# Linear attention and a gated feed-forward network: the written order of the steps is replaced from step 166 of 594 on

## The chip, the cores and the metric

The kernel runs on one core of one Trainium2 chip. The metric is the device time of one execution in microseconds (us); three runs of the kernel before gave 249.38, 249.55 and 249.58 us, median 249.55. The engines are named as the profile names them: PE (TensorE matmul), DVE (VectorE), ACT (ScalarE), POOL (GpSimd) and SP (SyncE, which here only issues transfers).

## The reference

Eight batches of linear attention with eight heads (576 tokens, head width 64), then a feed-forward network over all 4608 rows:

```python
phi = lambda x: np.where(x > 0, x, np.exp(x) - 1.0) + 1.0
kv  = einsum('bhsd,bhse->bhde', phi(k), v)
z   = sum(phi(k), axis=2)
x   = einsum('bhsd,bhde->bhse', phi(q), kv) / (einsum('bhsd,bhd->bhs', phi(q), z) + 1e-6)
x   = x.transpose(0, 2, 1, 3).reshape(4608, 512)
out = ((x @ w1) * (x @ w2)) @ w3 @ w_out      # w1, w2: 512 x 1024, w3: 1024 x 1024, w_out: 1024 x 512
```

## The kernel before

**Tiles and chunks.** The 576 tokens of a batch are 512 "full" tokens (four tiles of 128) and a tail of 64. The feed-forward part works on chunks of 512 rows: chunk c is the full tokens of batch c (0 to 7), and chunk 8 is the eight tails together. The product of w3 and w_out is made once, at the start, so a chunk needs only the two gate products, their elementwise product and one output product. The last three chunks (6, 8, 7) use a scheme with seven half-size products in place of eight, with more sums on DVE.

**The written order.** The program is not ordered by a scheduler. A string `ORDER` of 594 short steps (line 577 on) is walked once, and `step` turns each into its instructions. Each engine, and each queue of transfers, carries out its own instructions strictly in the order in which they were written, and waits at the first one whose input or buffer isn't ready. A step is a letter, a batch or chunk number, and a part:

- `L`, `M`, `N`: load one half (four heads, 512 KB of f32) of k, q, v of a batch (`load_qkv`, line 104). With a `+` it is issued by POOL, without by SP.
- `R`: load the tails of a batch (`load_tail`, line 114): `R4.0` is four transfers of 64 KB (q and k), `R4.1` two (v). `+` again means POOL.
- `x`/`X`, `y`/`Y`, `z`/`Z`: phi of k / of q, by an exponential on ACT (line 179), a maximum on DVE (line 184) and a minimum on DVE (lines 204, 209).
- `v`: v into bf16 (line 215; tails line 221), on ACT, or on DVE with `+`.
- `K`: the kv product of a batch, 18 matmuls (lines 245, 249) and two copies (line 254) on ACT, or on DVE with `+`.
- `T`: phi(q) turned round by a transposing transfer on SP (line 269). `D`: the same for the attention output of a batch (`D2.0`) or for the tails of two batches (`D1.1`) (line 351).
- `A`: the attention output of 128 tokens (part 4: the tail): four matmuls (line 310), then three instructions on DVE (lines 324 to 326). The four parts 0 to 3 of a batch fill the tile that `D` turns round.
- `F`: one of eight gate units of a chunk: eight matmuls (line 362), a copy on ACT (line 367), a product on DVE (line 368). `G`, `m`, `e`, `d`: the same for chunks 6, 8, 7 in the other scheme (lines 396 to 465).
- `O`: one output tile, eight matmuls (line 536) and a copy (line 538) on ACT, or on DVE with `+`. `S`, `H`: store of finished rows by SP (lines 546, 551). `Q`: the last output tile with its stores.

**Buffers that tie steps together.** `ld` has 13 buffers of one half each; four PSUM buffers serve the gate units (two for each `F`), two serve `O`, and a single one serves `K` and `A`, so that each of these waits until the one ahead of it has been read out. `ldr`, for tails, has three buffers. A transfer also waits for the eighth transfer ahead of it on its own queue to land.

**Gates.** `GATES` adds two waits by hand: `R6.0<T3.0` lets the q and k tails of batch 6 start only when `T3.0` has landed. It stands in both kernels.

```python
    for s in ORDER.split():
        step(s)
```

Of the kernel before, what the change touches and what calls it, by code (L numbers as in the profile page):

```python
# [20 lines left out]
def kernel(  # L21
# [568 lines left out]
    A3.0 O1.2 A3.2 L4.1 v4.2+ F2.6 A3.3 F2.3 N4.1 y4.0 F2.1 M4.0 x4.0 A3.1 x4.1 F2.0 M4.1 y4.2 v5.2+  # L590
    x4.2 F2.7 Y4.0 D3.0 F2.4 z4.0 F2.2 X4.1 Y4.1 S1.0 F2.5 v4.1 Z4.1 N4.0 M5.0 X4.0 Z4.0 A3.4 z4.2
    y4.1 O2.3 F3.7 z4.1 M5.1 v4.0 A2.4 Y5.0 F3.6 L5.0 T4.0 M6.1 R6.0+ x5.2 Y5.1 X5.0 F3.1 N5.1 Z5.0
    S1.1 O2.2+ K4 F3.2 M6.0 x6.2 X5.1 A4.2 Z5.1 F3.4 z5.2 F3.5 y5.0 A4.1 F3.0 L5.1 F3.3 N5.0 y5.1
    X6.1 y6.2 O2.1 A4.3 R6.1+ N6.0 S2.1 x5.1 N6.1 v5.0+ T5.0 O2.0 x5.0 v5.1+ A4.0 R7.0+ z5.1 D4.0
    z5.0 X6.0 O3.3 y7.2 O3.2+ K5+ S2.0 L6.0 z6.2 O3.1 A5.2 L6.1 O3.0 A5.1 D1.1 Y6.1 Z6.1 F4.2 A5.0
    Y6.0 F4.5 y6.1 F4.7 v6.0+ x6.1 L7.0 x6.0 M7.0 A5.3 D3.1 x7.0 z6.1 F4.0 v6.1+ v6.2 F4.6 A4.4 Z6.0
    F4.1 S3.0 F4.4 D5.0 A5.4 y6.0 z6.0 F4.3 M7.1 F5.7 x7.2 y7.0 Y7.0 z7.2 L7.1 N7.0 K6+ z7.0 F5.6
    F5.0 y7.1 X7.1 X7.0 Z7.0 F5.5 S3.1 F5.3 Y7.1 T6.0 R7.1+ Z7.1 A6.3 T7.0 F5.1 O4.2 A6.1 x7.1 O4.1
    A6.2 e1.0 e0.0 v7.0 F5.4 A6.0 z7.1 O4.3 e0.1 F5.2 e1.1 v7.2+ O4.0 N7.1 S4.1 e0.2 e0.3 e1.2 D6.0
    d6.0 v7.1 A6.4 e1.3 O5.1 O5.0 G6.1.1 G6.1.2 d6.1 G6.0.1 K7 d6.2 d6.3 G6.0.2 G6.0.3 m6.1.2 G6.0.4  # L600
    m6.0.2 S5.0 A7.3 G6.1.3 G6.0.5 G6.1.4 G6.1.5 m6.0.5 G6.2.4 G6.0.6 G6.0.7 G6.1.7 A7.0 G6.1.6
    G6.2.1 S4.0 G6.3.1 D5.1 G6.2.2 G6.2.3 G6.3.2 G6.3.3 m6.1.6 G6.2.5 G6.3.4 m6.2.2 G6.3.5 G6.2.6
    G6.2.7 A7.4 D7.1 G6.3.7 G6.3.6 O5.2 m6.3.5 A7.2 d8.0 O5.3 d8.2 G8.0.1 G8.0.4 m6.2.6 d8.1 m6.0.6
    d8.3 A7.1 G8.1.1 m6.3.6 G8.0.3 G8.0.2 G8.1.3 m6.2.5 G8.1.4 G8.0.5 G8.1.5 G8.3.4 G8.1.6 m8.0.2
    G8.0.7 G8.1.7 G8.2.4 m6.1.5 D7.0 G8.1.2 m8.0.5 d7.0 G8.2.1 S5.1 G8.3.1 G8.0.6 G8.2.3 m8.0.6
    G8.2.6 G8.3.3 G8.2.5 m6.3.2 G7.0.4 G8.3.5 G7.1.4 m8.1.2 G8.2.7 d7.1 G8.2.2 G8.3.7 d7.2 m8.1.5
    G8.3.6 O6.0 m8.3.5 m8.1.6 d7.3 O6.3 m8.2.5 O6.2+ m8.3.6 m8.2.6 O6.1 G7.0.1 m8.2.2 G8.3.2 G7.1.1
    m8.3.2 G7.0.3 S6.0 G7.0.6 G7.1.3 G7.0.5 G7.0.2 G7.1.5 G7.3.4 m7.1.5 G7.0.7 G7.2.4 m7.0.6 G7.1.7
    G7.1.6 m7.0.2 G7.2.1 G7.2.2 G7.3.1 S6.1 m7.2.2 G7.2.3 G7.2.6 G7.3.3 G7.2.5 G7.3.6 G7.3.5 G7.2.7
    G7.3.2 G7.1.2 G7.3.7 m7.3.2 m7.3.6 m7.1.2 O8.2 m7.3.5 O8.3 m7.0.5 O7.0 m7.2.6 O7.1 H8.2 m7.2.5  # L610
# [119 lines left out]
```

## Time and profile before

| what | value |
|---|---|
| three runs | 249.38, 249.55, 249.58 us |
| profiled execution, first to last instruction | 248.0 us |
| PE busy | 230.9 us (93%), 1548 matmuls |
| DVE busy | 187.4 us (76%), 434 instructions |
| ACT busy | 131.9 us (53%), 213 instructions |
| POOL busy | 49.4 us (20%) |
| DMA | 49.43 MB, mean 199 GB/s over the span |
| mean granted PE clock | 0.991 |

The profile gives for the profiled execution its span alone, 248.0 us, which is 1.5 us below the median of the runs. Its lines are read thus: a timeline row has the start in us, the duration in us, engine, line and operation, output<-input, the number of instructions merged into it, and in brackets the idle time ahead of it with what ended it. Rows of PE have a modelled end, so two rows that follow each other overlap a little: late matmuls are seen in the distance between starts. A row "SPq" is the time that SP spent in issuing a transfer; when the transfer landed stands in the view of the DMA issues. That view's last lines list, for the transfers issued in a stretch, how many there were, their size and the median time from issue to landing.

### The profile page before, as it was taken

The page shows a single profiled execution, that of the slowest core. Times are in us where ns is not written, and L with a number is a line of the kernel's source. Part 1 is how long each engine was busy: PE and PEld are TensorE (multiplying, and loading weights), DVE is VectorE, ACT ScalarE, POOL GpSimd, SP SyncE. Part 2 cuts the span into 40 slices and gives each one's busy share as a digit, 9 for nine tenths or more (in the row PEclk, how much of TensorE's full clock was granted, in tenths as well). Part 3 has the DMA queues.
Part 4 walks back from the last instruction along what each step waited for, and adds up shares of the span by engine and source line. Part 5 has one row for each costly group of instructions (what it writes and reads, how often), then busy time and mean ns, then how long its engine had stood idle before and what let it go on. Part 6 is the DMA issues. An engine that isn't in the chain of part 4 may idle for free.

```text
span 248.0 us, 4281 instructions
## 1 busy us (share of the span) xinstructions
PE 230.9 (93%) x1548; PEld 133.6 (54%) x1548; DVE 187.4 (76%) x434; ACT 131.9 (53%) x213; POOL 49.4 (20%) x79
## 2 busy tenths in 40 slices
PE   0699868999999999999999999999999999999994
PEld 0445455654454554345445544545488688578542
DVE  3227769777898847788768799988899999779810
ACT  2206667658756725675563383536466377245321
POOL 8546368665014050500000000000000000000000
PEclk9999988999999999999999999999999999999999
DMA  7999999999999999999999999917750133040144
GB/s 159 193 202 310 295 211 211 194 259 288 287 219 329 236 234 273 217 304 282 288 362 268 284 270 221 295 37 174 169 193 0 22 65 107 3 169 1 44 152 145
DMA packets 64021, 49.43 MB, mean 199 GB/s; under 512 B 32480, under 2 KB 58848, under 8 KB 64000
## 3 DMA queue, kind: packets, MB, share of 16 engines
q1 hardware_dynamic: 52928, 36.31, 58.3%
q0 software_dynamic: 10928, 12.72, 25.2%
q8 instruction: 12, 0.20, 0.3%
q10 hardware_dynamic: 144, 0.13, 0.2%
q14 instruction: 9, 0.07, 0.1%
HBM read 38.80 MB, written 9.44 MB: 194 GB/s over the span
## 4 chain that ended last, share of the span: by engine, by line
PE 67%; DMA 21%; ACT 3%; DVE 3%; SPq 2%; issue 2%; POOL 0%; ACTq 0%; DVEq 0%; POOLq 0%
PE o_ps L536 21%; PE a_ps L362 12%; PE b_ps L362 12%; DMA q<-in_q_dram 10%; PE gu L422 9%; DMA w3b<-in_moe_w_dram 7%; PE gt L422 6%; DMA k<-in_k_dram 4%; PE nd L310 3%; PE kvp L245 2%; SPq L104 1%; ACT e L179 1%; PE o_ps L561 1%; PE kvp L249 1%; DVE qj L209 1%
## 5 line engine op out<-in xcount | busy, mean ns | idle before, releaser
L536 PE MATMUL o_ps<-wf_sb,ab 128*128 128x512 bf16 x280 | 64.2, 379 | 0.0
L362 PEld LDWEIGHTS <-w_sb 128*128 128x128 bf16 x384 | 36.5, 98 | 40.6 <-issue 0.8
L362 PE MATMUL a_ps<-xt,w_sb 128*128 128x512 bf16 x192 | 50.3, 379 | 0.5 <-ACT a_sb L367 0.5
L362 PE MATMUL b_ps<-xt,w_sb 128*128 128x512 bf16 x192 | 50.3, 379 | 0.0
L536 PEld LDWEIGHTS <-ab 128*128 128x128 bf16 x280 | 26.8, 98 | 29.3
L368 DVE TENSOR_TENSOR ab<-a_sb,b_ps 128x512 bf16<-128x512 f32 x48 | 32.5, 683 | 11.5 <-PE b_ps L362 5.9
L538 ACT COPY o_sb<-o_ps 128x512 f32<-128x512 f32 x30 | 17.4, 585 | 42.8 <-PE o_ps L536 28.8
L367 ACT COPY a_sb<-a_ps 128x512 f32<-128x512 f32 x48 | 27.7, 585 | 22.2 <-PE a_ps L362 21.8
L326 DVE TENSOR_TENSOR xn<-nd,r 128x512 bf16<-128x512 f32 x30 | 20.7, 691 | 1.0
L422 PEld LDWEIGHTS <-spare 128*128 128x128 bf16 x192 | 18.7, 98 | 2.2
L179 ACT ACTIVATE e<-q 128x1024 bf16<-128x1024 f32 x16 | 16.8, 1057 | 5.7 <-DMA q<-in_q_dram 5.0
L310 PE MATMUL nd<-kv,qt 128*128 128x130 bf16 (+1 forms) x160 | 16.6, 228 | 2.9 <-ACT kv L254 1.8
L179 ACT ACTIVATE e<-k 128x1024 bf16<-128x1024 f32 x16 | 16.8, 1056 | 3.2 <-DMA k<-in_k_dram 3.1
L310 PEld LDWEIGHTS <-qt 128*128 128x128 bf16 (+1 forms) x160 | 11.8, 103 | 12.2 <-issue 3.5
L454 DVE TENSOR_TENSOR spare<-spare,gt 128x512 f32<-128x512 f32 x24 | 16.1, 680 | 1.8 <-PE gt L422 0.9
L154 PE MATMUL wf_ps<-wt_sb,w3t 128*128 128x512 bf16 x64 | 16.5, 403 | 0.6 <-DMA wt_sb<-in_moe_w_out_dram 0.6
L450 ACT COPY spare<-gu 128x512 f32<-128x512 f32 x24 | 13.6, 587 | 3.9 <-PE gu L422 3.7
L422 PEld LDWEIGHTS <-w_sb 128*128 128x128 bf16 x144 | 14.0, 98 | 2.7 <-issue 0.3
L465 DVE TENSOR_TENSOR ab<-spare 128x256 bf16<-128x256 f32 x36 | 14.1, 417 | 0.1
L114 POOL DMA_DIRECT2D qk32r<-in_q_dram x14 | 9.0, 644 | 23.3 <-ACT a_sb L367 10.7
L209 DVE TENSOR_TENSOR qj<-e,y 128x512 bf16<-128x512 bf16 x32 | 12.1, 418 | 2.0 <-ACT e L179 1.8
L422 PE MATMUL gu<-spare 128*128 128x256 bf16 x96 | 13.4, 272 | 0.0
(87 smaller groups left out, 294.0 us busy)
## 6 DMA issues: line engine op xcount, KB each, us to landing
out_dram<-o_sb SPq DMA_DIRECT2D x15, 512.0 KB, 3.9
q<-in_q_dram SPq DMA_DIRECT2D x13, 512.0 KB, 8.1
k<-in_k_dram SPq DMA_DIRECT2D x12, 512.0 KB, 7.0
v<-in_v_dram SPq DMA_DIRECT2D x12, 512.0 KB, 9.0
w3b<-in_moe_w_dram POOLq DMA_DIRECT2D x8, 256.0 KB, 10.0
k<-in_k_dram POOLq DMA_DIRECT2D x4, 512.0 KB, 9.1
w_sb<-in_moe_w_dram POOLq DMA_DIRECT2D x8, 256.0 KB, 7.5
q<-in_q_dram POOLq DMA_DIRECT2D x3, 512.0 KB, 12.6
```

The lines of the kernel that those rows point to most:

```text
L154: nc.tensor.matmul(wfs[i], w3ts[i][:, kc, :], wo_sb[:, kc, :], start=(kc == 0), stop=(kc == FC - 1))
L179: nc.scalar.activation(out=e, in_=x, func=AF.Exp)
L209: nc.vector.tensor_tensor(out=p[0][:, 2 * g + c].rearrange("p j u d -> p u j d"), in0=e[:, c], in1=y[:, c], op=ALU.min)
L310: nc.tensor.matmul(nds[g][rows, i * 2 * E1:(i + 1) * 2 * E1], w, kvs[b % 2][:, i, g].rearrange("p u e -> p (u e)"), start=True, stop=True)
L326: nc.vector.tensor_tensor(out=dst.rearrange("p (g h) e -> p g h e", g=2), in0=v4[:, :, :, 0:D], in1=r[rows].unsqueeze(3).to_broadcast([n, ...
L362: nc.tensor.matmul(ps, w[:, kc, f * P:(f + 1) * P], xt_of(c)[:, :, kc, :], start=(kc == 0), stop=(kc == KC - 1))
L367: nc.scalar.copy(out=a_sb, in_=a_ps)
L368: nc.vector.tensor_mul(out=abs_[c][:, f, :], in0=a_sb, in1=b_ps)
L422: nc.tensor.matmul(t[:, w], l, r, start=(first and w == 0 and k == 0), stop=(k == 1), skip_group_check=True)
L454: nc.vector.tensor_tensor(out=s, in0=o, in1=t, op=ALU.add)
L536: nc.tensor.matmul(o_ps, ab[:, f, m * P:(m + 1) * P], wf_sb[:, f, :], start=(f == 0), stop=(f == FC - 1))
L538: copy_of(alt)(out=rows_of(c, m // 2)[:, m % 2], in_=o_ps)
```

## The change

The first 165 steps stay as they are; they end with `F1.7 F1.6 x2.2`, the first two gate units of chunk 1 and the exponential of a tail. From there on the same 429 steps stand in another order. A few of them also change the engine: on ACT in place of DVE now run `v2.0 v5.0 v5.1 v6.0 v6.1`, the tails `v2.2 v4.2 v5.2 v7.2`, `O1.1` and the copies of `K5` and `K6`; on DVE in place of ACT run `v2.1`, `v3.2`, `v6.2`, `O2.3 O4.2 O5.0 O7.2`; the tails of batch 7 (`R7.0`, `R7.1`, six transfers) are issued by SP in place of POOL. All halves of q, k and v from batch 2 on are issued by SP in both kernels. PE has the same 1548 matmuls. The diff replaces the rows of the table from line 586 on; two of them of before, and two with the change:

```diff
-    A1.4 x2.1 F1.7 F1.6 x2.2 L2.0 y2.1 y2.2 Y2.0 x3.2 R3.1+ X2.0 O0.3 N2.1 x2.0 z2.1 N2.0 y2.0 z2.2
...
-    v3.1 S0.1 A2.1 y3.1 R5.1+ z3.0 z3.1 v3.0 v3.2 O1.1+ O1.0 T3.0 D2.0 S0.0 L4.0 K3 R4.1+ R4.0+ O1.3
...
+    A1.4 x2.1 F1.7 F1.6 x2.2 y2.2 z2.2 N2.1 y3.2 x3.2 O0.3 F1.0 Y2.0 X2.0 Z2.0 N2.0 y2.1 F1.1 v2.1+
...
+    T3.0 A2.1 R6.0+ v3.1 O1.1 z3.0 A2.0 O1.0 D2.0 R4.0+ S1.0 z3.1 K3 O1.2 A3.0 O1.3 A3.3 F2.5 F2.3
```

Three places of the order, engine by engine. Numbers behind a name tell buffers of one program apart, and are not the same in the two programs.

SP before, from the transpose of batch 2's attention output (`D2.0`) to that of batch 3 (`D3.0`). The loads are, in turn, both halves of k of batch 4, a half of its v, and both halves of its q:

```order
L351 DMA_TRANSPOSE xt_1149<-xn_1029 128x16x128
L546 DMA out_0_dram<-o_sb_1073 128x1024
L104 DMA k32_1152<-in_k_dram 128x4x256
L104 DMA k32_1223<-in_k_dram 128x4x256
L104 DMA v32_1263<-in_v_dram 128x4x256
L104 DMA q32_1280<-in_q_dram 128x4x256
L104 DMA q32_1308<-in_q_dram 128x4x256
L351 DMA_TRANSPOSE xt_1331<-xn_1195 128x16x128
L546 DMA out_0_dram<-o_sb_1135 128x1024
```

SP with the change, over the same stretch and to the fifth load behind it. The loads ahead of `D3.0` are one half of q of batch 5 and one of batch 4; behind it stand the other half of q of batch 4, a half of its v, both of its k, and the other half of its v:

```order
L351 DMA_TRANSPOSE xt_1142<-xn_1019 128x16x128
L546 DMA out_0_dram<-o_sb_1118 128x1024
L104 DMA q32_1262<-in_q_dram 128x4x256
L546 DMA out_0_dram<-o_sb_1182 128x1024
L104 DMA q32_1288<-in_q_dram 128x4x256
L351 DMA_TRANSPOSE xt_1304<-xn_1185 128x16x128
L104 DMA q32_1310<-in_q_dram 128x4x256
L104 DMA v32_1327<-in_v_dram 128x4x256
L104 DMA k32_1345<-in_k_dram 128x4x256
L104 DMA k32_1361<-in_k_dram 128x4x256
L104 DMA v32_1497<-in_v_dram 128x4x256
```

Five loads and a store stood between the two transposes; now there are two loads and two stores, and four of the five loads of batch 4 that stood there have moved behind the second transpose.

ACT before, from the copies of `O1.3` and `O1.2` through the gate units of chunk 2 (a_sb is the copy of a gate unit, e the exponential of a half, er that of a tail, vt a half of v):

```order
L538 COPY o_sb<-o_ps 128x512 x2
L367 COPY a_sb<-a_ps 128x512 x3
L179 ACTIVATE e<-k_1152 128x1024
L179 ACTIVATE e<-k_1223 128x1024
L367 COPY a_sb<-a_ps 128x512
L179 ACTIVATE er<-qk32r 128x512
L367 COPY a_sb<-a_ps 128x512 x3
L179 ACTIVATE e<-q_1308 128x1024
L367 COPY a_sb<-a_ps 128x512
L215 CAST vt_104<-v_1263 128x4x4x64
L179 ACTIVATE e<-q_1280 128x1024
```

ACT with the change, from the copies of `O1.2` and `O1.3` (the last two rows ahead of the gate units) through chunk 2 and into chunk 3:

```order
L538 COPY o_sb<-o_ps 128x512 x2
L367 COPY a_sb<-a_ps 128x512 x4
L179 ACTIVATE er<-qk32r 128x512
L367 COPY a_sb<-a_ps 128x512 x2
L221 CAST vr_106<-v32r 64x2x2x64 x2
L367 COPY a_sb<-a_ps 128x512 x2
L179 ACTIVATE e<-q_1262 128x1024
L367 COPY a_sb<-a_ps 128x512
L179 ACTIVATE e<-q_1310 128x1024
L179 ACTIVATE e<-q_1288 128x1024
L215 CAST vt_104<-v_1327 128x4x4x64
```

The exponentials of batch 4's halves stood among the eight copies of chunk 2; now only the tails of batch 4 (er and vr) stand there, and the first exponential of a half (one of batch 5's q) comes behind all eight.

POOL, the tails (each row is two transfers, or as many as its last number says). The piece of the difference begins at `R3.0`:

```order
 L114 DMA qk32r<-in_q_dram 64x4x64 x2
 L114 DMA qk32r<-in_k_dram 64x4x64 x2
-L114 DMA v32r<-in_v_dram 64x4x64 x2
-L114 DMA qk32r<-in_q_dram 64x4x64 x2
-L114 DMA qk32r<-in_k_dram 64x4x64 x2
-L114 DMA v32r<-in_v_dram 64x4x64 x6
+L114 DMA v32r<-in_v_dram 64x4x64 x4
 L114 DMA qk32r<-in_q_dram 64x4x64 x2
 L114 DMA qk32r<-in_k_dram 64x4x64 x2
 L114 DMA qk32r<-in_q_dram 64x4x64 x2
 L114 DMA qk32r<-in_k_dram 64x4x64 x2
```

Behind `R3.0` (its first two rows) stood `R3.1 R5.0 R2.1 R5.1 R4.1 R4.0` ahead of the gated `R6.0`; now only `R2.1 R3.1` do, and `R6.0` is followed by `R4.0 R5.1 R4.1 R5.0 R6.1`, which makes 18 transfers that wait behind the gate or are it.

More of the change, by code (lines that the diff above doesn't have):

```diff
@@ L585 @@
     M2.1 M3.1 A1.3 F0.3 P1.3 X2.1 R2.0+ A1.0 L2.1 h0 h1 Y2.1 P1.0 M2.0 h2 h3 Z2.1 i0 i1 X3.1 R3.0+
-    A1.4 x2.1 F1.7 F1.6 x2.2 L2.0 y2.1 y2.2 Y2.0 x3.2 R3.1+ X2.0 O0.3 N2.1 x2.0 z2.1 N2.0 y2.0 z2.2
-    Z2.0 F1.0 M3.0 R5.0+ y3.2 T2.0 v2.1 L3.0 Y3.1 R2.1+ F1.5 N3.1 v2.0+ z2.0 L3.1 Z3.1 v2.2+ O0.2
-    F1.2 F1.1 Y3.0 y5.2 z3.2 K2 F1.4 A2.2 X3.0 F1.3 A2.3 x3.0 O0.1 Z3.0 A2.0 x3.1 N3.0 y3.0 O0.0
-    v3.1 S0.1 A2.1 y3.1 R5.1+ z3.0 z3.1 v3.0 v3.2 O1.1+ O1.0 T3.0 D2.0 S0.0 L4.0 K3 R4.1+ R4.0+ O1.3
@@ L590 @@
[L590 to L610, printed above, removed]
@@ L611 @@
-    H8.3 O8.0 m7.1.6 S7.0 O8.1+ S8.0 O7.2 H7.2 Q7.3
+    A1.4 x2.1 F1.7 F1.6 x2.2 y2.2 z2.2 N2.1 y3.2 x3.2 O0.3 F1.0 Y2.0 X2.0 Z2.0 N2.0 y2.1 F1.1 v2.1+
+    R2.1+ z2.1 L2.0 y2.0 v2.2 F1.5 R3.1+ x2.0 z2.0 M3.0 v2.0 F1.4 O0.2 X3.0 K2 Y3.1 v3.2+ Z3.1 O0.1
+    Y3.0 Z3.0 T2.0 A2.3 F1.2 A2.2 N3.0 F1.3 v3.0 L3.1 z3.2 L3.0 x3.0 x3.1 y3.0 S0.1 y3.1 O0.0 N3.1
+    T3.0 A2.1 R6.0+ v3.1 O1.1 z3.0 A2.0 O1.0 D2.0 R4.0+ S1.0 z3.1 K3 O1.2 A3.0 O1.3 A3.3 F2.5 F2.3
+    A3.2 F2.0 M5.1 Y5.1 R5.1+ R4.1+ y4.2 S1.1 F2.2 M4.1 A3.1 R5.0+ D3.0 x4.2 z4.2 M4.0 F2.1 Y4.1
@@ new lines @@
+    N4.1 F2.4 R6.1+ L4.1 e0.0 A2.4 v4.2 L4.0 F2.6 e0.2 F2.7 X5.1 Z5.1 A3.4 F3.3 X4.0 Y4.0 Z4.0 O2.3+
+    X4.1 y5.2 v4.1 y4.1 F3.1 y6.2 Z4.1 x4.1 F3.4 z4.1 v5.2 y4.0 x4.0 F3.0 N4.0 z4.0 F3.5 v4.0 O2.2+
+    M5.0 X5.0 K4 v6.2+ e0.1 T4.0 F3.7 x5.2 z5.2 L5.1 x5.1 Y5.0 Z5.0 y5.1 F3.2 S0.0 A4.1 F3.6 L5.0
+    y5.0 O2.1 N5.0 x5.0 A4.0 v5.0 O2.0 z5.1 N5.1 S2.1 A4.2 T5.0 v5.1 O3.3 z5.0 A4.3 D4.0 O3.2+ K5
+    S3.1 O3.1 A5.3 M6.1 O3.0 A5.0 F4.0 X6.1 A5.2 F4.7 M6.0 X6.0 Y6.0 Z6.0 D3.1 F4.2 F4.4 A5.1 F4.5
@@ new lines @@
+    e1.0 F4.3 L6.1 y6.1 x6.1 A4.4 R7.0 L6.0 y6.0 y7.2 D5.0 F4.1 x6.0 F4.6 z6.0 Y6.1 Z6.1 F5.6 x6.2
+    z6.2 z6.1 F5.5 N6.1 v6.1 N6.0 A5.4 e1.1 e1.3 M7.0 X7.0 F5.7 S2.0 F5.4 Y7.0 O4.2+ v6.0 K6 O4.3
+    T6.0 A6.3 S3.0 O4.0 A6.1 F5.3 D5.1 x7.2 z7.2 A6.0 M7.1 Y7.1 R7.1 X7.1 Z7.1 N7.0 v7.0 L7.0 F5.1
+    F5.0 A6.2 L7.1 Z7.0 F5.2 x7.1 y7.1 O4.1 y7.0 A6.4 e0.3 x7.0 z7.0 S4.1 z7.1 O5.0+ v7.2 N7.1 v7.1
+    D6.0 d6.2 O5.1 K7 d6.0 d6.1 d6.3 G6.1.1 e1.2 T7.0 G6.0.1 G6.0.2 G6.1.2 m6.0.2 G6.1.3 G6.0.3
+    G6.1.4 A7.3 S4.0 G6.0.4 G6.0.5 G6.1.5 S5.0 G6.2.4 G6.0.6 G6.0.7 G6.1.6 G6.1.7 m6.1.6 A7.0 m6.0.6
@@ new lines @@
+    G6.2.1 G6.2.2 G6.3.1 G6.2.3 G6.3.2 G6.3.3 G6.2.5 G6.3.4 G6.2.6 G6.3.5 G6.2.7 A7.4 G6.3.6 G6.3.7
+    O5.2 m6.3.2 D1.1 A7.2 O5.3 m6.1.2 m6.2.6 D7.1 d8.0 d8.1 d8.3 G8.0.1 G8.0.2 d8.2 A7.1 G8.1.1
+    G8.0.3 m6.3.6 G8.0.4 G8.1.3 G8.0.5 m8.0.5 G8.1.4 m6.2.5 G8.3.4 S5.1 D7.0 G8.1.5 G8.0.7 m6.2.2
+    G8.2.4 G8.0.6 m8.0.6 G8.1.7 O6.0 m6.3.5 m6.1.5 m6.0.5 O6.3 d7.2 G8.2.1 G8.2.2 m8.2.2 d7.0 G8.3.1
+    G8.2.3 G8.1.6 G8.3.3 G8.2.5 G8.3.2 G7.0.4 G8.3.5 G8.2.7 G8.3.6 m8.3.6 m8.1.6 G7.1.4 G8.3.7
+    m8.0.2 O6.2+ S6.1 d7.1 d7.3 O6.1 S6.0 m8.2.5 G7.0.1 m8.3.5 G8.1.2 m8.1.5 m8.1.2 G7.1.1 G7.0.3
@@ L612 @@
+    G7.0.6 G7.1.3 G7.0.5 G7.2.4 G7.1.5 G8.2.6 G7.0.7 G7.1.6 G7.1.7 G7.0.2 m8.2.6 m8.3.2 m7.1.6
+    G7.2.1 G7.2.2 G7.3.1 G7.2.3 G7.3.2 m7.0.5 G7.3.4 G7.3.3 G7.2.5 G7.3.6 G7.3.5 G7.2.7 G7.1.2
+    G7.2.6 G7.3.7 m7.0.2 m7.2.5 O8.2 O8.3 m7.3.2 H8.3 m7.3.5 m7.2.2 O8.0 m7.1.2 m7.0.6 O8.1+ H8.2
+    S8.0 O7.0 O7.1 S7.0 m7.2.6 m7.3.6 m7.1.5 O7.2+ H7.2 Q7.3
     """
```

## The prediction

> **What bounds the kernel now.** I read the busy times by stage first, then the chain of waits, then the rows around each gap of PE. By stage (length, PE, PE's weight loads, DVE, ACT, POOL with their counts, granted clock, DMA share, GB/s):
>
> ```profile
> 60.00:95.00 35.00, 35.00 (x209) 17.71 (x208) 26.69 (x65) 21.73 (x35) 8.61 (x14) 1.00 1.09 261
> 95.00:130.00 35.00, 33.80 (x185) 16.02 (x184) 28.05 (x63) 21.44 (x32) 3.94 (x6) 1.00 1.10 289
> 130.00:243.00 113.00, 112.99 (x774) 70.64 (x775) 94.64 (x215) 56.23 (x100) 0.00 (x0) 1.00 0.54 138
> ```
>
> From 60 us on, where the new order begins, PE is never idle but for 1.2 us between 95 and 130. PE keeps its 1548 matmuls, so a new order can save what PE loses here and no more, while it can lose any amount. The chain of waits leaves PE only where it lies on loads:
>
> ```profile
> 91.59 12.85 DMA q<-in_q_dram
> 118.44 9.40 DMA k<-in_k_dram
> ```
>
> The gaps, as starts of neighbouring PE rows:
>
> ```profile
> 98.05 1.03 PE L362 MATMUL a_ps<-xt,w_sb 128*128 128x512 bf16 x4
> 98.92 1.03 PE L362 MATMUL b_ps<-xt,w_sb 128*128 128x512 bf16 x4
> 100.45 1.02 PE L362 MATMUL a_ps<-xt,w_sb 128*128 128x512 bf16 x4 [0.51 <-ACT a_sb L367]
> 108.67 1.03 PE L362 MATMUL b_ps<-xt,w_sb 128*128 128x512 bf16 x4
> 109.92 0.41 PE L310 MATMUL nd<-kv,qt 128*64 128x130 bf16 x4 [0.22 <-DVE xnr L326]
> 127.62 1.89 PE L536 MATMUL o_ps<-wf_sb,ab 128*128 128x512 bf16 x8
> 129.99 0.40 PE L310 MATMUL nd<-kv,qt 128*128 128x130 bf16 x4 [0.47 <-DVE xn L326]
> ```
>
> Four wide matmuls take 0.87 us (98.05 to 98.92), eight 1.73. So PE is late by 100.45 - 99.79 = 0.66, by 109.92 - 109.54 = 0.38 and by 129.99 - 129.35 = 0.64 us: 1.68 us together. Who made it late stands on ACT and DVE:
>
> ```profile
> 98.87 1.06 ACT L179 ACTIVATE e<-k 128x1024 bf16<-128x1024 f32 x1 [1.77 <-DMA k<-in_k_dram]
> 99.83 0.57 ACT L367 COPY a_sb<-a_ps 128x512 f32<-128x512 f32 x1
> 104.47 1.06 ACT L179 ACTIVATE e<-q 128x1024 bf16<-128x1024 f32 x1 [0.65 <-DMA q<-in_q_dram]
> 107.94 0.76 DVE L209 TENSOR_TENSOR qj<-e,y 128x512 bf16<-128x512 bf16 x2 [0.55 <-ACT e L179]
> 127.86 0.69 DVE L184 TENSOR_SCALAR y<-k 128x1024 bf16<-128x1024 f32 x1 [1.24 <-DMA k<-in_k_dram]
> ```
>
> In all three a half of k or q (of batch 4, 4 and 5) landed after its reader had come up in ACT's or DVE's order, and a gate unit's copy or the division of an attention tile, which PE needed, stood behind that reader. So the kernel is bound by PE, and its waste is late loads.
>
> **Term 1, the three late loads: -1.7.** Gaps one and two came from batch 4. With the change four of its five halves there are issued behind `D3.0`, and their exponentials stand behind all copies of chunk 2, so ACT no longer meets them between the gate units. Are they then late for `K4`? Steps on PE have these lengths:
>
> ```profile
> 85.66 0.62 PE L245 MATMUL kvp<-vt,kj 128*128 128x130 bf16 x8
> 86.78 1.89 PE L536 MATMUL o_ps<-wf_sb,ab 128*128 128x512 bf16 x8
> 88.74 1.89 PE L536 MATMUL o_ps<-wf_sb,ab 128*128 128x512 bf16 x8
> 90.69 1.03 PE L362 MATMUL a_ps<-xt,w_sb 128*128 128x512 bf16 x4
> ```
>
> `K` is 1.12 (85.66 to 86.78), `O` and `F`, eight wide matmuls each, 1.73, and `A` the 0.23 that the rows at 86.78 and 88.74 leave between them; a tail's `A` has the same four matmuls. From `A3.1` to `K4` the new order has `F2.1 F2.4 A2.4 F2.6 F2.7 A3.4 F3.3 O2.3 F3.1 F3.4 F3.0 F3.5 O2.2`, which is 11 x 1.73 + 3 x 0.23 = 19.7 us. The loads behind `D3.0` start when it has been issued. Before, `A3.1` and `D3.0` stood here, and the last of the five transfers behind `D3.0` was a half of k with 9.4 us to landing (last row, from the view of the DMA issues):
>
> ```profile
> 96.10 0.39 PE L310 MATMUL nd<-kv,qt 128*128 128x130 bf16 x4
> 98.66 5.40 SPq L351 DMA_TRANSPOSE xt<-xn  x1
> 106.81 0.71 SPq L104 DMA_DIRECT2D k<-in_k_dram  x1
> k<-in_k_dram SPq DMA_DIRECT2D x1, 512.0 KB, 9.4
> ```
>
> Five transfers behind `D3.0` thus landed by 116.2, 20.1 us after `A3.1` began, with `D3.0` itself slow. A `D3.0` without a queue ahead (below: 4.3 in place of 8.9 us) gives 15.5 us, and 1.1 us for the cast of v leaves 3 of the 19.7 us. Bounds: 0 to 1.5 us late. I take 0, since the loads that made `D3.0` slow are the ones that moved.
>
> Gap three came from `L5.1`, the fifth transfer behind `T4.0` (`M6.1 N5.1 S1.1 M6.0 L5.1`). The new order there is `L5.1 S0.0 L5.0 N5.0 N5.1`: it is the first, and lands four transfers sooner. Its cover is wide; I take the whole 0.64.
>
> **Term 2, the turned attention outputs: +0.4.** This is what the change gives up. Chunk c's first `F` needs `D`, which needs the last `A` of its batch. The last `A` of batch 5, the issues of `D2.0`, `D4.0` and `D5.0`, and the time to landing of `D2.0`, `D3.0`, `D4.0`, `D5.0`:
>
> ```profile
> 144.12 0.39 PE L310 MATMUL nd<-kv,qt 128*128 128x130 bf16 x4
> 85.08 1.65 SPq L351 DMA_TRANSPOSE xt<-xn  x1
> 133.41 2.08 SPq L351 DMA_TRANSPOSE xt<-xn  x1
> 147.13 3.78 SPq L351 DMA_TRANSPOSE xt<-xn  x1
> xt<-xn SPq DMA_TRANSPOSE x1, 4.7
> xt<-xn SPq DMA_TRANSPOSE x1, 8.9
> xt<-xn SPq DMA_TRANSPOSE x1, 4.3
> xt<-xn SPq DMA_TRANSPOSE x1, 5.9
> ```
>
> With the last `A` at 81.98 (next fence), 96.10, 129.99 and 144.12, the way from `A` to the landing took 7.8, 11.5, 7.7 and 8.9 us; for batch 2, PE had 8.7 us of steps to cover it (81.98 to 90.69). In the new order PE has less: `A2.0 O1.0 K3 O1.2 A3.0 O1.3 A3.3`, 7.0; `A3.1 F2.1 F2.4 A2.4 F2.6 F2.7 A3.4`, 7.6; `A4.3 O3.2 K5 O3.1 A5.3 O3.0 A5.0`, 7.0; `A5.1 F4.5 F4.3 A4.4 F4.1 F4.6`, 7.4. If each way stays as long, PE waits 0.8 + 3.9 + 0.7 + 1.5 = 6.9 us. The shortest way is the division on DVE and the quickest of these transfers, `D4.0`'s 4.3:
>
> ```profile
> 81.98 0.39 PE L310 MATMUL nd<-kv,qt 128*128 128x130 bf16 x4
> 82.84 0.69 DVE L326 TENSOR_TENSOR xn<-nd,r 128x512 bf16<-128x512 f32 x1
> ```
>
> 83.53 - 81.98 = 1.55, and 4.3, is 5.9 us: nowhere late, with 1.1, 1.7, 1.1 and 1.5 to spare. What lengthens a way is the queue ahead of it. `D3.0` took 8.9 us behind five loads and a store; now two loads and two stores stand there, issued well before. `D4.0` stood right behind `N6.0 S2.1 N6.1 T5.0`; now no load of batch 6 is ahead of it. `D5.0` still has a crowd: `S3.1 M6.1 M6.0 D3.1 L6.1 R7.0 L6.0`. All are nearer to the short end; I take 0.2 for `D5.0`, 0.1 for each of `D3.0` and `D4.0`.
>
> **Term 3, batch 3's last half: +0.1.** `N3.1` now stands behind `S0.1`, fifth behind `T2.0`. Before, the fifth was `S0.1`:
>
> ```profile
> 73.75 1.07 SPq L546 DMA_DIRECT2D out_dram<-o_sb  x1
> out_dram<-o_sb SPq DMA_DIRECT2D x1, 512.0 KB, 11.4
> ```
>
> It landed at 85.2. With 1.05 us for the cast (below), `K3`, whose steps ahead on PE are the same set (85.66), would be up to 0.6 late. But six tails (`R4`) went out among those five and have moved away. 0 to 0.6; I take 0.1.
>
> **Terms at nothing.** Net, DVE gives four casts of halves of v and some smaller copies to ACT, and takes three output tiles from it:
>
> ```profile
> L215 DVE CAST vt<-v 128x1024 bf16<-128x1024 f32 x5 | 3.4, 687 | 0.0
> L215 ACT CAST vt<-v 128x1024 bf16<-128x1024 f32 x7 | 7.3, 1052 | 0.7 <-DMA v<-in_v_dram 0.6
> ```
>
> The casts take 4 x 0.69 = 2.7 us off DVE and put 4 x 1.05 = 4.2 us onto ACT. Both lie under PE: in the stages above ACT is busy at most 62% and DVE 84%. Without that cover the 4.2 us would count, so they are the price if ACT's order puts them ahead of a copy that PE needs; I count neither this nor a gain from DVE, for which PE waited only when a load was late. `R7` on SP costs six more issues of about half a microsecond (as the store's and load's rows above), in a stretch in which SP waits for finished tiles.
>
> **The sum.** The profiled execution's span is 248.0 us, 1.5 below the median of the runs; I keep that 1.5. So 249.55 - 1.68 + 0.4 + 0.1 = 248.4 us, and about 246.9 of span.
>
> **Rivals.** *A, the turned outputs come late* (slower). If the ways keep half of what they would be late by, PE waits 3.4 us at the starts of chunks 2 to 5 in place of 0.4: 249.55 - 1.7 + 3.4 + 0.1 = 251.4. It decides once these four waits sum to over 1.6. For it: each cover shrinks by 1.7 us or more, and even the old way of batch 2, the least crowded, would be 0.8 late. Against: fewer transfers ahead.
>
> *B, the tails' burst.* `R4.0` now waits behind the gated `R6.0`; 18 tails then go out in a row, beside `D2.0` and halves of q. The median of such tails to landing:
>
> ```profile
> qk32r<-in_q_dram POOLq DMA_DIRECT2D x14, 64.0 KB, 7.1
> ```
>
> The gate opens when `T3.0`, issued just ahead of `D2.0`, lands: between 85.08 and 89.8, I take 87. POOL's 14 issues between 60 and 95 took 8.61 us, 0.62 each, so `R4.0`'s last leaves at 92 and lands, 7.1 later, at 99. Its reader `y4.2` comes up on DVE behind `F2.0` and one maximum: 85.66 + 1.12 + 5 x 1.73 + 3 x 0.23 + 2 x 0.69 = 97.5. DVE would wait 1.6 us with the division of `A3.1` behind it, so `D3.0` goes that much later: +1.0 with its spare partly used, 249.4. Against: fewer loads beside the tails. The Trainium skill, "DMA: Bandwidth & Descriptors", section "Queues, rings and completion order", says that each DMA engine takes the queues with work in turn, a packet at a time. By it the tails would not wait behind SP's loads (18 x 64 KB at 261 GB/s is 4.4 us of transfers), but `D2.0` and `D3.0` would share with them: less of B, and at most those 4.4 us more of A, an estimate. No run here shows the two apart.
>
> *C, the late loads only move.* The five halves of batch 4 now leave in one burst and are read in one piece; if one of them stops ACT or DVE as before, the 1.7 is not won: 249.5. For it: loads come in the order of their readers, with 3 us of cover at most. Against: no copy of chunk 2 stands behind such a reader any more.
>
> **How the numbers follow.** Forecast 0.60, A 0.18, B 0.10, C 0.12. The forecast's own range is 247.6 to 249.0. Down to 247.3 I allow for gaps that the modelled ends of PE rows hide; up to 251.0 takes in B, C and the nearer half of A, so about 0.1 is left out above. A measurement of this kernel tells 0.2% (0.5 us: 249.05 to 250.05) from no change. Faster: nearly all of the forecast and a quarter of B and C, 0.62. Same: half of B and C and a little of the forecast, 0.14. Slower: A and the rest, 0.24.
>
> **What would show it.** In the changed profile: no gap of PE among the gate units of chunk 2, none ahead of `A2.4` and of batch 4's last `A`; `D3.0` landing in 5 to 6 us in place of 8.9; the first `F` of chunks 2 to 5 waiting at most 0.3 us. I am wrong if PE waits over 1 us at such a first `F`, if DVE waits at a tail's maximum near 96 us, or if the gaps of PE after 60 us sum to more than 1.7 us.

## The result and the profile after

With the change the kernel takes 0.9939 of the time before (95% interval 0.9919 to 0.9959): 248.5 us median of 20 runs, against 249.97 us for 20 runs of the kernel before beside them. A second comparison later gave 0.995 (0.9918 to 0.9981). The profiled execution took 247.36 us, its span 245.6 us. The busy times by stage, as they were shown of before (length, PE, weight loads, DVE, ACT, POOL, clock, DMA share, GB/s):

```profile
60.00:95.00 35.00, 35.00 (x210) 17.70 (x208) 25.10 (x60) 21.60 (x36) 6.47 (x11) 1.00 0.89 235
95.00:130.00 35.00, 35.00 (x195) 17.04 (x194) 31.62 (x71) 24.09 (x37) 4.66 (x8) 1.00 0.98 272
130.00:243.00 113.00, 111.99 (x774) 70.48 (x771) 89.57 (x202) 58.50 (x104) 0.00 (x0) 1.00 0.57 153
```

The 1.2 us that PE lost between 95 and 130 are gone (33.80 before, 35.00 now); the last stage holds less because PE ends sooner. DMA moves less in the first two stages (235 and 272 GB/s in place of 261 and 289) and more behind them. The timeline of PE and ACT at the three places where gaps stood:

```profile
95.40 1.03 PE L362 MATMUL a_ps<-xt,w_sb 128*128 128x512 bf16 x4
96.27 1.03 PE L362 MATMUL b_ps<-xt,w_sb 128*128 128x512 bf16 x4
97.13 0.39 PE L310 MATMUL nd<-kv,qt 128*128 128x130 bf16 x4
97.36 1.02 PE L362 MATMUL a_ps<-xt,w_sb 128*128 128x512 bf16 x4
127.69 1.89 PE L536 MATMUL o_ps<-wf_sb,ab 128*128 128x512 bf16 x8
129.42 0.39 PE L310 MATMUL nd<-kv,qt 128*128 128x130 bf16 x4
96.95 0.63 ACT L179 ACTIVATE er<-qk32r 128x512 bf16<-128x512 f32 x1
98.42 0.58 ACT L367 COPY a_sb<-a_ps 128x512 f32<-128x512 f32 x1 [0.84 <-PE a_ps L362]
```

The gate units of chunk 2 follow each other at 0.87 us a half, and the last attention tile of batch 4 comes 1.73 us after the output tile ahead of it: nothing is late. ACT's copy at 98.42 now waits for PE, where before PE waited for such a copy. The sum of all distances between starts beyond the issue rate, after 60 us, is 3.44 us before and 1.66 now, 1.78 us less. What is left is about 0.09 us at each side of a tail's attention, in both kernels, and two places of 0.1 us.

That is not the whole difference of the two profiles. PE's last matmul starts 2.52 us sooner, 0.73 of them already at `F1.7`, the first gate unit of chunk 1 and the third last of the 165 shared steps. So the table below, of all kernels run, has for each profile the start of `F1.7` and the span less that start, which holds the part in which the orders differ. The ratio is of all runs of a kernel; the last two columns are of the one execution that was profiled.

| kernel | ratio to before, interval | F1.7 starts | span less that |
|---|---|---|---|
| before, two profiles | 1 | 59.33, 58.23 | 188.7, 188.5 |
| changed, two profiles | 0.9939, 0.995 | 58.59, 58.79 | 187.0, 187.6 |
| engine choices alone | 1.0051 (1.0021 to 1.0082) | 59.34 | 188.9 |
| order alone | 1.0166 (1.0135 to 1.0197) | 58.94 | 192.4 |
| L5.1 first | 1.0006 (0.9973 to 1.0039) | 60.32 | 189.6 |
| readers later | 1.0011 (0.9977 to 1.0044) | 59.37 | 188.4 |
| both | 1.0015 (0.9984 to 1.0047) | 59.32 | 189.6 |
| seven steps moved | 1.0091 (1.0051 to 1.013) | 60.65 | 188.5 |
| four loads back | 1.029 (1.0252 to 1.0329) | 58.67 | 195.6 |
| one load back | 0.9961 (0.9926 to 0.9996) | 58.42 | 187.5 |
| tails late | 1.0174 (1.0129 to 1.022) | 58.57 | 191.5 |
| batch 6 early | 1.0091 (1.0056 to 1.0127) | 61.25 | 189.7 |

### The profile page after: what moved, and what is told of

It is laid out like the page before. It is cut to its first block, busy times and chain, and to the rows that moved or that the text cites. A ratio compares the mean times of both kernels' runs of the same rounds, so it can differ in the third digit from the quotient of the medians.

```text
span 245.6 us, 4278 instructions
## 1 busy us (share of the span) xinstructions
PE 229.7 (94%) x1548; PEld 133.2 (54%) x1548; DVE 184.7 (75%) x425; ACT 136.4 (56%) x222; POOL 44.8 (18%) x73
## 4 chain that ended last, share of the span: by engine, by line
PE 83%; DMA 13%; ACT 2%; issue 1%; POOL 0%; ACTq 0%; POOLq 0%
PE o_ps L536 25%; PE a_ps L362 17%; PE b_ps L362 17%; PE gu L422 9%; PE gt L422 6%; DMA q<-in_q_dram 5%; DMA k<-in_k_dram 5%; PE nd L310 4%; DMA wt_sb<-in_moe_w_out_dram 3%; PE kvp L245 2%; ACT e L179 1%; PE o_ps L561 1%; PE kvp L249 1%; PE xtp L341 1%; POOL w3b L137 0%
## 5 line engine op out<-in xcount | busy, mean ns | idle before, releaser
L538 ACT COPY o_sb<-o_ps 128x512 f32<-128x512 f32 x27 | 15.6, 586 | 34.6 <-PE o_ps L536 24.9
L310 PE MATMUL nd<-kv,qt 128*128 128x130 bf16 (+1 forms) x160 | 15.9, 221 | 2.8 <-DVE xn L326 1.7
L310 PEld LDWEIGHTS <-qt 128*128 128x128 bf16 (+1 forms) x160 | 11.5, 99 | 11.6 <-DVE xn L326 3.0
L114 POOL DMA_DIRECT2D qk32r<-in_q_dram x12 | 7.6, 636 | 33.5 <-ACT o_sb L538 30.9
L324 DVE TENSOR_SCALAR r<-nd 128x8 f32<-128x8 f32 (+1 forms) x38 | 6.1, 162 | 10.0 <-PE nd L310 9.9
```

The lines of the kernel that those rows point to most:

```text
L310: nc.tensor.matmul(nds[g][rows, i * 2 * E1:(i + 1) * 2 * E1], w, kvs[b % 2][:, i, g].rearrange("p u e -> p (u e)"), start=True, stop=True)
L538: copy_of(alt)(out=rows_of(c, m // 2)[:, m % 2], in_=o_ps)
```

## Experiments: a part of the change alone

**The engine choices without the order.** The 19 choices between DVE and ACT, in the old order:

```diff
-v2.0+
+v2.0
...
-O2.3
+O2.3+
...
-O5.0
+O5.0+
```

> The order of before, with the 19 choices between DVE and ACT that the change makes (R7 stays on POOL), and no step moved. Theory (late loads, so the order of loads and readers, made the gain): the three gaps of PE after 60 us stay, 1.4 to 2.0 us together as in before (1.68); time 0.997 to 1.003 of before. Rival (DVE, which is 2.7 us lighter, made the gain): the gaps shrink to half or less, time below 0.997 of before.

The gaps stayed, in other places: 0.07 us ahead of `A2.4`, 0.83 at 130 us, 0.12 at chunk 4, and a new one of 0.77, in the timeline of PE:

```profile
180.61 0.60 PE L422 MATMUL gt<-xt,w_sb 128*128 128x256 bf16 x4
181.82 0.60 PE L422 MATMUL gu<-xt,w_sb 128*128 128x256 bf16 x4 [0.61 <-DVE o_sb L538]
```

The copy of `O5.0`, moved to DVE, keeps PE waiting there. The lighter DVE is not the gain; in the old order the choices cost something: 1.0051 lies above the theory's 1.003, though its interval reaches below that, and the profile's part behind `F1.7` is only 0.2 to 0.4 us longer than before's. The first gap did not come up here, although no step was moved for it; the second profile of the kernel before, below, lacks it too, so which of the marginal loads is late changes from one execution to another.

**The order without the engine choices.** The same 19 steps put back in the new order:

```diff
-v2.0
+v2.0+
...
-K5
+K5+
...
-v6.0 K6
+v6.0+ K6+
```

> The changed order with the choices between DVE and ACT of before (19 steps go back, R7 stays on SP). Theory (the gain is the order's alone, the engine choices give nothing): no more than 0.4 us of gaps beside those of the changed kernel, 0.993 to 0.996 of before. Rival (the order needs the lighter DVE): DVE comes late to divisions or gate products, gaps of 0.8 us or more, 0.997 or more.

The rival was right: 1.0166. PE waits at nine places: 0.57 us at `K2`, 0.70 at `K3`, 0.69 at chunk 2, 1.06 at four places between 127 and 135 us, 0.32 at `K7`, and the largest, 2.08, at `K6` (timeline of PE and DVE):

```profile
162.75 1.03 PE L536 MATMUL o_ps<-wf_sb,ab 128*128 128x512 bf16 x4
165.69 0.63 PE L245 MATMUL kvp<-vt,kj 128*128 128x130 bf16 x8 [1.91 <-DVE vt L215]
164.94 0.69 DVE L215 CAST vt<-v 128x1024 bf16<-128x1024 f32 x1
```

The cast of v, back on DVE, ran from 164.94, behind work of DVE that had no pause since at least 154.8, and `K6` had to wait for it. So the order and the choices are one change: each alone is slower than before.

## Experiments: repairing the late loads in the old order

**One load first.**

```diff
-T4.0 M6.1 R6.0+
+T4.0 L5.1 M6.1 R6.0+
...
-F3.0 L5.1 F3.3
+F3.0 F3.3
```

> The order of before with one step moved: the load L5.1 (a half of k of batch 5) goes from behind F3.0 to right behind T4.0. Theory (gap three is L5.1 landing late, and nothing else is late there): the gap of 0.64 us ahead of the last attention tile of batch 4 is gone or under 0.1 us, the gaps at chunk 2 (0.66 and 0.38 us) stay; 0.6 us won, about 0.9974 of before. Rival (late loads only move): the four transfers that are now behind it make another reader late, and a gap of 0.3 us or more opens elsewhere between 120 and 145 us; 0.999 to 1.002.

**Three readers later.**

```diff
-A3.1 x4.1 F2.0
+A3.1 F2.0
...
-F2.2 X4.1 Y4.1 S1.0 F2.5 v4.1 Z4.1 N4.0
+F2.2 x4.1 Y4.1 S1.0 F2.5 X4.1 v4.1 N4.0
...
-A3.4 z4.2
+A3.4 Z4.1 z4.2
```

> The order of before with three readers moved and no load: the exponential of batch 4's half of k (x4.1) from among the first gate units of chunk 2 to behind F2.2, its X4.1 behind F2.5, and the minimum of q's half (Z4.1) behind the tail's attention A3.4. Theory (a gap is a reader that stands ahead of work PE needs; moving it suffices): the gaps ahead of the third gate unit and ahead of A2.4 go (0.66 and 0.38 us), the one at 130 us stays; 1.0 us won, 0.996 of before. Rival (the loads have to be moved too, since what is late at chunk 2 is the landing itself): the readers are late at their new places, gaps of 0.6 us or more stay between 95 and 120 us; 0.999 to 1.002.

**Both together.**

> The two edits above together: four steps of 429 moved. Theory (the three late loads are the whole of the change's gain): 1.4 to 1.7 us won, 0.993 to 0.995 of before, which is the time of the changed kernel (0.9939) to within the intervals. Rival (the rest of the new order earns a part of the gain, or holds off a loss): at most 1.0 us won, 0.996 or more.

By their times all three landed on the rival's side: no gain that could be measured (the interval of `L5.1` alone just reaches the theory's 0.9974). The third gap is in all four profiles of the old order with `L5.1` at its old place (0.40 to 0.89 us) and in none of the three with it moved (these two and the next run). What the readers' edit did for the gaps at chunk 2 is not shown: they are missing with `L5.1` alone as well, where nothing was done for them. Other waits took their place, though not those that the rivals of the first two runs named. With both, PE's timeline and the row of `D3.0` in the DMA issues read:

```profile
105.40 1.90 PE L536 MATMUL o_ps<-wf_sb,ab 128*128 128x512 bf16 x8
108.63 1.04 PE L362 MATMUL a_ps<-xt,w_sb 128*128 128x512 bf16 x4 [1.33 <-DMA xt<-xn]
147.79 0.41 PE L310 MATMUL nd<-kv,qt 128*64 128x130 bf16 x4
148.69 1.02 PE L362 MATMUL a_ps<-xt,w_sb 128*128 128x512 bf16 x4 [0.48 <-ACT a_sb L367]
150.03 1.02 PE L362 MATMUL b_ps<-xt,w_sb 128*128 128x512 bf16 x4 [0.32 <-ACT a_sb L367]
147.10 1.06 ACT L179 ACTIVATE e<-k 128x1024 bf16<-128x1024 f32 x1 [1.26 <-DMA k<-in_k_dram]
```

```profile
xt<-xn SPq DMA_TRANSPOSE x1, 10.3
```

The first gate unit of chunk 3 now waits for `D3.0`, 1.49 us in starts (108.63 less 105.40 and 1.73). The turned output was late all along, behind the same loads; before, PE came to it late because of its gaps at chunk 2 and didn't notice. At 148 us ACT comes to a half of k of batch 7 sooner than it lands, and holds up a gate unit's copy: 0.55 and 0.48 us. With `L5.1` alone these were 1.27, 0.54 and 0.49 us, with the readers alone 1.0 us at chunk 3 and 0.4 at 130.

**Seven steps moved.** The places that this run named were mended too, with three more steps moved (the expectation's nine counts `X4.1` and `Z4.1` twice):

```diff
-Y4.0 D3.0 F2.4
+Y4.0 D3.0 M4.1 F2.4
...
+A3.4 X4.1 z4.2
...
+F3.7 Y4.1 z4.1 Z4.1 M5.1
...
+F4.4 x7.0 D5.0
```

> The order of before with nine steps moved: the four of the two edits together, and then what that run showed to be late next. One half of q of batch 4 (M4.1), the last of the five loads ahead of D3.0, goes behind D3.0, its readers X4.1, Y4.1 and Z4.1 behind it; and the exponential of a half of k of batch 7 (x7.0) goes behind F4.4. Theory (a gap is a load whose way lies too long for its place, and once each late one that the traces name has room, the gain is there): D3.0 lands 6 to 7.5 us after its issue in place of 8.6 to 10.3, the first gate unit of chunk 3 waits 0 to 0.3 us in place of 1.5, no gap at F4.1, and 1.2 to 1.8 us are won: 0.993 to 0.996 of before. Rival (loads stay late as long as the same bytes have to pass in this stretch; each mended place shows another): gaps of 0.8 us or more stay somewhere between 95 and 165 us, 0.998 or more.

The named waits went as the theory had it (`D3.0` landed 7.7 us after its issue), but the rival had the result: PE waited elsewhere, the largest for a transposing transfer of phi(q) of batch 4, whose last input (`Z4.1`) had been moved:

```profile
117.81 1.03 PE L362 MATMUL b_ps<-xt,w_sb 128*128 128x512 bf16 x4
119.26 0.40 PE L310 MATMUL nd<-kv,qt 128*128 128x130 bf16 x4 [0.42 <-DMA qt<-qj]
```

With 0.58 here, 0.31 at `K5` and 0.21 at chunk 5, the distances beyond the issue rate sum to 3.34 us, as much as before (3.44). The ratio of 1.0091 is worse than this profile explains, in which the part behind `F1.7` has before's length; that is left open.

## Experiments: undoing a part of the changed kernel

**Four loads back ahead of `D3.0`.**

```diff
-F2.2 M4.1 A3.1 R5.0+ D3.0
+F2.2 M4.1 M4.0 N4.1 L4.1 L4.0 A3.1 R5.0+ D3.0
```

> The changed kernel with four loads of batch 4 (M4.0, N4.1, L4.1, L4.0) moved back ahead of D3.0, their readers left in place. Theory (the queue ahead of the transposing transfer sets its way): D3.0 lands 8 to 10 us after its issue in place of 4.5, the first gate unit of chunk 3 waits 2 to 4 us, and the kernel takes 0.8 to 1.5% more than the changed one, 1.002 to 1.009 of before. Rival (the way of D3.0 is set by something else, such as the loads that run beside it from other queues): it still lands in under 6 us, no wait, 0.994 of before.

**One load back.**

```diff
-F2.2 M4.1 A3.1 R5.0+ D3.0
+F2.2 M4.1 M4.0 A3.1 R5.0+ D3.0
```

> The changed kernel with one load (M4.0, half of q of batch 4) moved back ahead of D3.0, where four moved back cost 5.7 us at the first gate unit of chunk 3. Theory (D3.0 lands 2 to 4.5 us after the last load ahead of it, and loads land 1.5 us apart): M4.0 lands at 101 to 103, D3.0 at 104.5 to 107, PE waits 0 to 2 us for it: 0.994 to 1.003 of before. Rival (the cost of a load ahead is a matter of four or more at once): D3.0 lands by 104.2, no wait.

The theory held: the loads ahead of `D3.0` set its way, by which from here on its time from issue to landing is meant. With four loads all of its sizes were too small, 11.5 us in place of 8 to 10 for the way, 5.6 in place of 2 to 4 for the wait, 1.029 in place of 1.009 at most. Timeline of SP and PE, the DMA issues, and the busy times of two short stretches, all with four loads back:

```profile
99.94 9.59 SPq L351 DMA_TRANSPOSE xt<-xn  x1
105.53 0.41 PE L310 MATMUL nd<-kv,qt 128*64 128x130 bf16 x4
111.53 1.89 PE L362 MATMUL a_ps<-xt,w_sb 128*128 128x512 bf16 x4 [5.58 <-DMA xt<-xn]
113.20 1.91 PE L362 MATMUL b_ps<-xt,w_sb 128*128 128x512 bf16 x4
114.91 2.33 PE L536 MATMUL o_ps<-wf_sb,ab 128*128 128x512 bf16 x7
```

```profile
xt<-xn SPq DMA_TRANSPOSE x1, 11.5
```

```profile
111.50:116.40 4.90, 4.88 (x12) 1.76 (x13) 1.18 (x2) 2.95 (x4) 0.00 (x0) 0.52 0.59 200
116.40:130.00 13.60, 13.60 (x77) 6.76 (x76) 11.12 (x25) 9.97 (x16) 0.00 (x0) 1.00 0.57 140
```

`D3.0` held SP for 9.59 us and landed 11.5 us after its issue; PE stood 5.6 us longer than the usual distance behind a tail. Then the granted clock was 0.52 for 4.9 us: four wide matmuls took 1.71 us (113.20 to 114.91) in place of 0.87, which costs 2.5 us more on 12 matmuls. With one load back, `D3.0` took 6.5 us and PE waited 0.55. That is too little for the times to tell: 0.9961 (0.9926 to 0.9996) and the changed kernel's 0.995 overlap:

```profile
104.63 0.41 PE L310 MATMUL nd<-kv,qt 128*64 128x130 bf16 x4
105.53 0.82 PE L362 MATMUL a_ps<-xt,w_sb 128*128 128x512 bf16 x3 [0.48 <-DMA xt<-xn]
```

Put in order over all profiles, the way of `D3.0` follows the loads that SP issued ahead of it and that had not landed when it was issued (a load that landed within 0.25 us of the issue is not counted):

| loads not landed | way of `D3.0`, us |
|---|---|
| 0 | 4.5 (changed), 4.3 (tails late), 4.3 (batch 6 early) |
| 1 | 5.4 (changed, second profile), 6.5 (one back), 4.4 (order alone) |
| 2 | 7.7 (seven steps) |
| 3 | 8.9 and 8.8 (before), 8.3, 10.0, 10.2, 10.3 (its four variants) |
| 5 | 11.5 (four back) |

The tails on POOL's queue do not set it: eight of them had not landed at the issue in the changed kernel (4.5 us), none with the tails late (4.3).

**The tails of batch 4 last.**

```diff
-R4.0+ S1.0
+S1.0
...
-R5.1+ R4.1+ y4.2
+R5.1+ R4.1+ R5.0+ R6.1+ R4.0+ y4.2
...
-A3.1 R5.0+ D3.0
+A3.1 D3.0
...
-F2.4 R6.1+ L4.1 e0.0
+F2.4 L4.1 e0.0
```

> The changed kernel with the q and k tails of batch 4 (R4.0) moved from second to last among the tails behind the gate (R6.0 R5.1 R4.1 R5.0 R6.1 R4.0), still ahead of their reader y4.2: rival B of the prediction, made worse on purpose. Theory (B's mechanism holds, and the changed order is only on the safe side of it, by 1.4 us of landing): R4.0's last tail lands at 98.5 to 101 us in place of 95.7, DVE waits for it 1.5 to 3.5 us ahead of the division of A3.1, D3.0 goes that much later, and after its spare of 1.5 us PE waits 0 to 2 us: 0.994 to 1.001 of before. Rival (DVE has slack there): no wait of PE over 0.2 us, 0.993 to 0.995 of before.

Rival B's mechanism is real and dear: 1.0174, where the theory had 1.001 at most. `R4.0` landed at 102.74 in place of 95.65, later than expected: POOL issues nothing from 92.6 to 94.8 us, because the eighth transfer ahead on its queue hasn't landed, and `R4.0` now stands behind that stop; in the changed kernel, where the stop is from 92.5 to 94.6, it stands ahead. DVE and PE:

```profile
96.83 0.69 DVE L184 TENSOR_SCALAR y<-q 128x1024 bf16<-128x1024 f32 x1
102.93 0.43 DVE L184 TENSOR_SCALAR yr<-qk32r 128x512 bf16<-128x512 f32 x1 [5.41 <-DMA qk32r<-in_k_dram]
99.42 1.03 PE L362 MATMUL a_ps<-xt,w_sb 128*128 128x512 bf16 x4
104.01 1.02 PE L362 MATMUL b_ps<-xt,w_sb 128*128 128x512 bf16 x4 [3.56 <-DVE ab L368]
```

What stopped PE was not `D3.0` but the gate unit ahead: the product on DVE that empties its PSUM buffer stood behind the maximum that waited. The profiled execution is the fastest of this kernel's six (251.9 us, median 254.3), so its wait accounts for a part of the median's loss only; the rest is open.

**Batch 6 as early as before.** In the changed order its halves of q and v are loaded 16 to 29 us later than they were:

```diff
-T4.0 F3.7
+T4.0 M6.1 F3.7
...
-S0.0 A4.1
+S0.0 M6.0 A4.1
...
-N5.0 x5.0
+N5.0 N6.0 x5.0
...
-N5.1 S2.1
+N5.1 N6.1 S2.1
```

> The changed kernel with the four halves of q and v of batch 6 loaded where before loaded them, among the loads of batch 5 (M6.1 behind T4.0, M6.0 behind S0.0, N6.0 behind N5.0, N6.1 behind N5.1), their readers left in place. Theory (part of the gain is that 2 MB less has to pass between 115 and 130 us): L5.0, N5.0 and N5.1 land 2 to 5 us later, the maximum of L5.0 and the cast of N5.1 wait for them, K5 or an attention tile of batch 4 waits 1.5 to 4 us: 1.000 to 1.010 of before. Rival (only the order around D3.0 and of L5.1 counts): waits of PE under 0.5 us, 0.993 to 0.997.

The theory held: PE waited 0.60, 0.96 and 0.95 us for attention divisions and an output copy, of which the second is

```profile
129.91 0.69 DVE L184 TENSOR_SCALAR y<-k 128x1024 bf16<-128x1024 f32 x1 [0.60 <-DMA k<-in_k_dram]
131.70 0.40 PE L310 MATMUL nd<-kv,qt 128*128 128x130 bf16 x4 [0.80 <-DVE xn L326]
```

This is gap three again, with the other half of batch 5's k. So it is a condition of the gain that these 2 MB don't pass between 115 and 130 us: with them, the new order loses 2.5 us to three waits there. (Of the 5.4 us by which this run's span is longer than the changed kernel's, 2.7 stand ahead of `F1.7`.)

## Experiments: both kernels once more

> The kernel before once more, for a second profile. Theory (the 0.73 us by which the changed kernel's profile is ahead at the end of the 165 shared steps is what differs from execution to execution): PE reaches the first gate unit of chunk 1 anywhere from 58.6 to 60.7 us. Rival (the changed steps act on the shared ones): at 59.3 us or later, as in each profile of the order of before so far (59.3 to 60.7), where each with the changed order had 58.6 to 58.9. From there on gaps of PE of 1.4 to 2.1 us over those of the changed kernel's profile, at chunk 2 or at the first gate unit of chunk 3, and at 130 us.

> The changed kernel once more, for a second profile and a second ratio. Theory (the waits of PE that it lacks are lacking in every execution): no single wait of PE over 0.3 us after 60 us, and 0.992 to 0.996 of before. Rival (the first profile was a lucky one): a wait of 0.5 us or more at a first gate unit or at K4, or a ratio of 0.997 or more.

The kernel before took 248.59 us in its single run; its PE reached `F1.7` at 58.23 us, sooner than any other profile: the 0.73 us at the shared steps were execution to execution, as the theory had it. Its gaps, in PE's timeline:

```profile
106.47 1.04 PE L362 MATMUL a_ps<-xt,w_sb 128*128 128x512 bf16 x4 [0.26 <-DMA xt<-xn]
126.10 1.89 PE L536 MATMUL o_ps<-wf_sb,ab 128*128 128x512 bf16 x8
128.72 0.40 PE L310 MATMUL nd<-kv,qt 128*128 128x130 bf16 x4 [0.73 <-DVE xn L326]
```

This time nothing was late among chunk 2's gate units; `D3.0` cost 0.43 us at chunk 3, `A2.4` was 0.09 late, and gap three was 0.89 (128.72 less 126.10 and 1.73): 1.4 us together, in place of 1.68.

The changed kernel was not free of waits in its second profile. The theory's limit of 0.3 us for a single wait failed, though not at the places that the rival named (timeline of PE and ACT):

```profile
93.64 0.39 PE L310 MATMUL nd<-kv,qt 128*128 128x130 bf16 x4
94.48 1.02 PE L362 MATMUL a_ps<-xt,w_sb 128*128 128x512 bf16 x4 [0.46 <-ACT a_sb L367]
92.87 1.07 ACT L538 COPY o_sb<-o_ps 128x512 f32<-128x512 f32 x2 [5.63 <-DMA out_dram<-o_sb]
```

The copy of `O1.2` on ACT waits until the store `S1.0` has landed and frees its buffer (92.77 us here, 91.86 in the first profile), and two gate copies stand behind it: 0.62 us. The same wait is in three variants with this order (0.65, 0.37 and 0.69 us) and missing in two, so it is in four of the seven profiles with this order. The ratio, 0.995, lies in the theory's range.

## Why the prediction was right, and where it was not

**The bound** held: PE, late by loads. **Term 1** (-1.7) holds for the profile shown (-1.78), with all three gaps gone and none at `K4`, whose loads landed by 112.24 us, 5 us ahead of it. Over two profiles of each kernel it is smaller: 1.55 us of gaps before and 0.3 after, and the parts behind `F1.7` differ by 1.3 us on average (188.6 and 187.3), which is the measured 0.5 to 0.6%. The step that was too narrow was to take three gaps of one execution as the kernel's: the loads around `D3.0` are late as a body, and which reader shows it changes. The prediction's sign of no gap among the gate units of chunk 2 fails in the second profile, where a late store, which the prediction had not put down, holds up ACT.

**Term 2** (+0.4) was mis-sized; it measured 0. The reason was right: what lengthens a way is the queue ahead. The ways in the first profile are 5.0, 4.5, 4.4 and 4.3 us:

```profile
xt<-xn SPq DMA_TRANSPOSE x1, 5.0
xt<-xn SPq DMA_TRANSPOSE x1, 4.5
xt<-xn SPq DMA_TRANSPOSE x1, 4.4
xt<-xn SPq DMA_TRANSPOSE x1, 4.3
```

They left 0.4 us at chunk 2 (landed 89.58, first gate unit 90.00), 1.5 at chunk 3, 1.0 at chunk 4 and 0.9 at chunk 5. PE's cover at chunk 3 was 8.0 us and not 7.6, since a tail's attention takes 0.35 us with 0.1 ahead of it, and not the 0.23 of a full tile. I had priced `D5.0` by its crowd; that had landed before it was issued, or was far on its way. One load more ahead of `D3.0` would have made the term right (0.55 us).

**Term 3** (+0.1) measured 0: `N3.1` landed at 81.25, 3.7 us ahead of `K3`.

**The sum** came out closer than its terms: 248.4 us against 248.5. Over two profiles term 1 was about 0.4 us too large, terms 2 and 3 together 0.5, and the two errors offset each other. That part of the agreement is luck.

**The terms at nothing** came out as nothing, for a wrong reason. I took the engine choices as free because both engines lie under PE by their busy shares. The order alone, with those choices undone, is 1.7% slower: with the change DVE is busy 90% between 95 and 130 us (31.62 of 35), and has no room there for casts of 0.69 us at the wrong places; the largest loss, at `K6`, lies behind that stage, in a stretch in which DVE had no pause. They were a condition of term 1. (The issues of `R7` were put at half a microsecond; the rows named for it say 1.07 and 0.71, and the four of `R7.0` took 0.62 to 1.16 us on SP. No wait of PE shows for it.)

**The rivals.** A did not occur, and needed more loads at `D3.0`. B did not occur by 1.35 us: `R4.0` landed at 95.65, its reader came up at 97.00 without a wait (timeline of DVE):

```profile
97.00 0.46 DVE L184 TENSOR_SCALAR yr<-qk32r 128x512 bf16<-128x512 f32 x1
```

I had it landing at 99, since the gate opened at 85.46 and not at 87, and its tails took 5.0 to 6.1 us and not 7.1. The run with the tails last shows that the case was rightly on the list and priced too low. C, that late loads only move, is what every partial repair of the old order showed, and not the change itself.

## What to carry to other kernels

A load that is late is seldom alone: before repairing the reader that shows it, count what lies unfinished in the queue when the next transfer that the bound engine needs is issued, and move those loads behind it. A repair that removes one wait is judged by the end of the span, not by the wait, and an order and its engine choices are judged together. Where two profiles share a beginning, subtract it before comparing.

## What was not expected of the hardware

PE reached `F1.7`, near the end of the 165 steps that are the same in all 14 profiles, at 58.23 to 61.25 us; runs of the unchanged kernel went from 247.76 to 251.92 us. That is more than the effect of the change, which shows only in medians of many runs and in the part behind the shared steps.

After a wait of 5.6 us PE's granted clock was 0.52 over the next 4.9 us; after one of 3.6 us, with the tails late, it was 1.00. The Trainium skill, "TensorE: Matmul & The Clock Gate", section "Part 1: The HAM clock gate (the "warmup" mystery)", has the clock halved after a whole idle window of about 3.4 us and restored after a busy one; the windows run free, so 3.6 us need not hold a whole one. The runs agree.
